# Reordering the start-up of a fused retention and gMLP kernel: the first v, the bias, the gain, the norms and the first fillers

## The chip, the cores and the metric

The kernel runs on one core of one Trainium2 chip. The metric is the device time of one execution in microseconds, as the median of several executions. The core has five engines that run side by side and wait for each other by semaphores: PE (TensorE, matmul; its weight loads are listed as PEld), DVE (VectorE), ACT (ScalarE), POOL (GpSimd) and SP (SyncE, which here only issues DMAs). Each engine works through its own instructions in program order. DMAs are issued from the instruction streams of SP, ACT and POOL.

## What is computed

Inputs q, k and v have 8 batches, 8 heads, 576 positions and 64 columns a head, in float32. First comes retention, a causal attention without softmax, in which each head h decays with its own gamma; then a gMLP block over the joined heads (512 columns):

```python
scores = scale * np.matmul(q, k.transpose(0, 1, 3, 2))
gamma = 1.0 - 2.0 ** (-5.0 - np.arange(H, dtype=np.float32))
Dmat = np.where(rel >= 0, gamma[:, None, None] ** rel[None, :, :], 0.0)
x = np.matmul(scores * Dmat[None], v)          # heads joined: (8, 576, 512)
...
h = gelu(x @ w_in)                             # tanh form, 1024 columns
u, v = h[..., :512], h[..., 512:]
v_n = (v - mu) / np.sqrt(var + 1e-06) * g_ln
v_s = np.einsum('ts,bsd->btd', w_sg, v_n) + b_sg[None, :, None]
out = x + (u * v_s) @ w_out
```

So each position needs a normalized row v_n, the 576 positions of a batch are then mixed by w_sg with the bias b_sg, and the gated result goes through w_out.

## The kernel before

**Blocks.** The work is cut into 18 blocks j, two groups of four batches with nine blocks each. The first block of a group (j = 0 and 9) holds the first 64 positions of its four batches; each of the other eight holds 256 positions of one batch, so that each batch has two blocks. A block has two chunks c of 128 rows.

**Names.** For a block, in the order of the data:

- load(j) (line 76) issues the DMAs of k, q and v. For j = 0 each of the three is four transfers of 128 KB, one for each batch, and for x >= 2 they go out on ACT's queue instead of SP's. Three buffers of each kind are there (pool ld), so load(j + 3) waits for the casts of block j.
- cast(j, part, engine) (247) scales k or q by the decay and writes them in bfloat16, or copies v: kb, qb, vb (klead, vlead for a leading block).
- T(j, part) (266) transposes k or q on PE; ACT copies kT, DVE copies qT out of PSUM.
- Sc(j, g) (283) forms half of the masked scores; DVE multiplies by the mask (tile ret).
- Z(j, c) (305) adds a chunk to the running state of keys and values (zp, copied to zb); inter(j) (327) multiplies the queries by that state, intra(j) (340) adds the product of scores and v; ACT and DVE copy the result, transposed, into xT.
- V(j, c) (361) projects a chunk by the second half of w_in (hv) and ACT applies gelu (vg). Its norm has three steps, kept as functions: stats (374: mean and variance, rs, and vc = (vg - mean) * g on DVE), power (371: rs to the power -1/2 on POOL) and norm (388: vn = vc * rs on ACT; for the leading rows two halves, vnm). Ahead of the loop they are called by hand as stats_of[n], pow_of[n] and norm_of[n] with n = 2 * j + c; in the loop they follow two and four steps later by themselves.
- U(j, c) (407) projects by the first half of w_in and applies gelu (uT).
- W(b, c, half) (420) mixes the positions of batch b by w_sg: five matmuls over the four vn of that batch and the vnm, then a product with uT on DVE (gT). It can end only when all norms of its batch are there. O(p, m) (439) multiplies by w_out, adds x and stores 128 rows.

**Constants.** split_b (168) clears the two bias tiles wL and splits b_sg into three bfloat16 parts (bp); place_b(e) (188) sends these into wL[e] by three small DMAs of POOL's; fill_first (184) and fill_consts (179) set constant halves of vnm; load_w(j) (193) loads w_sg in five pieces, and for j = SB w_out, on POOL's queue; build_wT (200) transposes w_sg; build_g (216) spreads g_ln over all rows by a matmul with a column of ones (gp, copied by ACT to g_bc). spin(n) (224) issues n matmuls on a tile of zeros that nobody reads.

**Order.** The order is written out by hand: lines 480 to 597 interleave blocks 0 to 2 with the constants and start block 3, and from line 602 a loop over j = 3 to 17 goes on: block j's intra, V and U, the scores of block j + 1, the transposes of j + 2, the casts of j + 3 and the loads of j + 4.

**Fillers.** W and O are not called at fixed places. release(j) (465) runs at the end of the second block of a batch and queues that batch's 8 W and 4 or 5 O in the list wo, behind the first two entries still in it and mixed with the rest; run(n) (460) executes the next n entries, if there are any. The loop has four such places for each block (line 601), 3 to 6 entries a block in all. What is left after the loop runs at the end (642).

Of the kernel before, what the change touches and what calls it, by code (L numbers as in the profile page):

```python
# [19 lines left out]
def kernel(  # L20
# [12 lines left out]
    nc = tc.nc  # L33
# [10 lines left out]
    SB = (S + 127) // 128  # L44
# [31 lines left out]
    def load(j, parts=(k, q, v)):  # L76
        if j not in loaded:
            loaded[j] = ld.tile([128, 2, H, 2, D], F32, name="qk"), ld.tile([128, H, 2, D], F32, name="vf")
        qk, vf = loaded[j]
        gr, b, half = place(j)  # L80
        for dst, src in ((qk[:, 1], k), (qk[:, 0], q), (vf, v)):
            if src not in parts:
                continue
            if b is None:
                for x in range(GB):
                    eng = nc.scalar if j == 0 and x >= 2 else nc.sync
                    eng.dma_start(dst[32 * x:32 * x + 32], src[GB * gr + x, :, :LEAD, :].rearrange(
                        "h (p a) d -> p h (a d)", a=2))
            else:
                s0 = LEAD + 256 * half  # L90
                nc.sync.dma_start(dst[:], src[b, :, s0:s0 + 256, :].rearrange("h (p a) d -> p h (a d)", a=2))
# [76 lines left out]
    def split_b():  # L168
        nc.gpsimd.memset(wL[0][64:], 0.0)
        nc.gpsimd.memset(wL[1][:64], 0.0)  # L170
        rest = bs
        for n in range(3):
            nc.gpsimd.tensor_copy(bp[:, n, :], rest[:])
            if n < 2:
                left = w3.tile([SB * 2, 64], F32, name="left")
                nc.gpsimd.tensor_tensor(left[:], rest[:], bp[:, n, :], op=Alu.subtract)
                rest = left

    def fill_consts():
        for x in (1, 2):  # L180
            nc.gpsimd.memset(vnm[x][0][64:], 1.0)
            nc.gpsimd.memset(vnm[x][1][:64], 1.0)

    def fill_first():
        nc.gpsimd.memset(vnm[0][0][64:], 1.0)
        nc.gpsimd.memset(vnm[0][1][:64], 1.0)

    def place_b(e):
        for n in range(3):
            r = 64 * (1 - e) + n  # L190
            nc.gpsimd.dma_start(wL[e][r:r + 1, :], bp[:SB * 2 - 1, n, :] if e else bp[1:, n, :])

    def load_w(j):
        if j == SB:
            nc.gpsimd.dma_start(w_out[:], moe_w_out.rearrange("(c p) f -> p c f", p=128))
            return
        n = min(128, S - 128 * j)
        nc.gpsimd.dma_start(wnat[:n, j, 64:64 + S], moe_w_sg[128 * j:128 * j + n, :])
# [17 lines left out]
    def build_g():  # L216
        gp = psD.tile([128, F2], F32, name="gp", tag="d")
        nc.tensor.matmul(gp[:], one[:], grow[:], start=True, stop=True)
        nc.scalar.copy(g_bc[:], gp[:])
# [4 lines left out]
    def spin(n):  # L224
        for _ in range(n):
            nc.tensor.matmul(idle[:], fill[:, :128], fill[:], start=True, stop=True)  # L226
# [20 lines left out]
    def cast(j, part, eng):  # L247
        s = blk.setdefault(j, {})
        qk, vf = loaded[j]
        b, half = place(j)[1:]  # L250
        kind = 0 if b is None else 1 + half
        if part == "q":
            dst, src, tab = w2.tile([128, 2, H, D], BF, name="qb"), qk[:, 0], gq
        else:
            pool = consts if b is None else w3
            dst = pool.tile([128, 2, H, D], BF, name=part + ("lead" if b is None else "b"))
            src, tab = (qk[:, 1], gk) if part == "k" else (vf[:], None)
        s[part + "b"] = dst
        o = dst[:].rearrange("p a h d -> p h a d")
        if tab is None:  # L260
            copy(eng, o, src)
        else:
            eng.tensor_tensor(o, src, tab[:, kind].rearrange("p a h -> p h a").unsqueeze(3).to_broadcast(  # L263
                [128, H, 2, D]), op=Alu.mult)
# [40 lines left out]
    def Z(j, c):  # L305

        gr, b, half = place(j)
        if b is None or (half, c) == (1, 1):
            nb = GB * gr if b is None else b + 1
            if c == 0 or nb == GB * (gr + 1):  # L310
                return
            src, lo, n, first = blk[NPG * gr], 32 * (nb % GB), 32, True
            zcur[0] = psZ.tile([128, KK, D], F32, name="zp")
        else:
            src, lo, n, first = blk[j], 64 * c, 64, False
        z, rows = zcur[0], slice(lo, lo + n)
        for a in range(2):
            for kk in range(KK):
                for r in range(2):
                    h = 2 * kk + r  # L320
                    nc.tensor.matmul(z[64 * r:64 * r + 64, kk, :], src["kb"][rows, a, h, :], src["vb"][rows, a, h, :],  # L321
                                     start=(first and a == 0 and kk == 0), stop=True, skip_group_check=True)
        zb = w3.tile([128, KK, D], BF, name="zb")
        copy(nc.scalar if j < 3 else nc.vector, zb[:], z[:])
        zbs[(j, 1) if c == 0 else (j + 1, 0)] = zb

    def inter(j):
        s = blk[j]
        qT = s["qT"]
        s["ot"] = ot = [psO.tile([128, KK, 2, 64], F32, name="ot") for _ in range(2)]  # L330
        if place(j)[1] is None:
            return
        for kk in range(KK):
            for c in range(2):
                for r in range(2):
                    rr = slice(64 * r, 64 * r + 64)
                    nc.tensor.matmul(ot[c][rr, kk], zbs[j, c][rr, kk, :], qT[rr, :, kk, 64 * c:64 * c + 64],  # L337
                                     start=(kk == 0), stop=False, skip_group_check=True)
# [20 lines left out]
    stats_of, pow_of, norm_of = {}, {}, {}  # L359
# [47 lines left out]
    def U(j, c):  # L407
        p, m = chunk(j, c)
        if p not in uTs:
            uTs[p] = pairp.tile([128, KK, NT * 128], BF, name="uT")  # L410
        hu = psD.tile([128, KK, 128], F32, name="hu", tag="d")
        for c in range(KK):
            for kk in range(KK):
                nc.tensor.matmul(hu[:, c, :], w_in[:, kk, 128 * c:128 * c + 128],  # L414
                                 xTs[p][:, kk, 128 * m:128 * m + 128],
                                 start=(kk == 0), stop=(kk == KK - 1), skip_group_check=True)
        nc.scalar.activation(uTs[p][:, :, 128 * m:128 * m + 128], hu[:], Act.Gelu_apprx_tanh)  # L417
        tick()
# [41 lines left out]
    def run(n):  # L460
        for _ in range(n):
            if wo:
                wo.pop(0)()

    def release(j):
        b, half = place(j)[1:]
        if b is None or half == 0:
            return
        ws = [lambda b=b, c=c, h=h: W(b, c, h) for h in range(2) for c in range(KK)]
        os = wo[2:]  # L470
        del wo[2:]
        while ws or os:
            wo.extend(ws[:2] + os[:1])
            ws, os = ws[2:], os[1:]
        p, e = divmod(b, 2)
        for m in ([MID] if e else []) + [(MID + 1) * e + x for x in range(MID)]:
            wo.append(lambda p=p, m=m: O(p, m))
# [2 lines left out]
    HEAD = 3  # L480
    spin(16)
    build_masks()
    split_b()
    cast(0, "k", nc.vector)
    T(0, "k")
    spin(2)
# [1 line left out]
    T(0, "q")  # L488
    spin(3)
    cast(0, "v", nc.gpsimd)  # L490
    place_b(0)
    Sc(0, 0)
    Sc(0, 1)
    Z(0, 1)
# [5 lines left out]
    intra(0)  # L500
    load(3)
    nc.gpsimd.memset(wnat[:, :, 0:64], 0.0)
    cast(1, "q", nc.vector)
    spin(3)
    V(0, 0, None)
    V(0, 1, None)
    T(1, "k")
    T(1, "q")
    cast(1, "v", nc.gpsimd)
    build_g()  # L510
    Sc(1, 0)
    Z(1, 0)
    cast(2, "k", nc.gpsimd)
# [16 lines left out]
    V(1, 1, None)  # L530
    Z(2, 0)
    inter(2)
    stats_of[0]()
    place_b(1)
    cast(3, "k", nc.gpsimd)
    fill_first()
    pow_of[0]()
    Sc(2, 1)
    Z(2, 1)
    wb = ["L0", "L1"] + list(range(SB - 1))  # L540
    U(0, 0)
    stats_of[2]()
    U(0, 1)
    intra(2)
    U(1, 0)
    stats_of[3]()
    pow_of[2]()
    norm_of[0]()
    norm_of[2]()
    V(2, 0, None)  # L550
    V(2, 1, None)
    cast(3, "q", nc.gpsimd)
    load_w(SB)
    load(5)
    build_wT(wb[0])
    cast(3, "v", nc.gpsimd)
    U(1, 1)
    build_wT(wb[1])
    stats_of[4]()
    pow_of[3]()  # L560
    fill_consts()
    pow_of[4]()
    norm_of[3]()
    build_wT(wb[2])
    U(2, 0)
    build_wT(wb[3])
# [4 lines left out]
    U(2, 1)  # L571
    build_wT(wb[5])
    norm_of[5]()
    T(3, "k")
    T(3, "q")
    release(2)
    cast(4, "k", nc.gpsimd)
    cast(4, "q", nc.gpsimd)
    cast(4, "v", nc.gpsimd)
    load(6)  # L580
    run(1)
    Sc(3, 0)
    Z(3, 0)
    run(1)
# [7 lines left out]
    cast(5, "q", nc.gpsimd)  # L592
    cast(5, "k", nc.gpsimd)
    cast(5, "v", nc.gpsimd)
    later(14, stats_of[1])
    later(16, pow_of[1])
    later(18, norm_of[1])
# [75 lines left out]
```

## Time and profile before

| | us |
|---|---|
| median of three executions | 238.41 (238.07 to 238.46) |
| the profiled execution | 236.13 |
| its span, first to last instruction | 234.4 |
| PE busy | 219.7 (94%) |
| DVE busy | 164.2 (70%) |
| ACT busy | 134.7 (57%) |
| POOL busy | 130.6 (56%) |
| moved by DMA | 41.58 MB, 177 GB/s on the mean |

The profiled execution is one of its own, faster by 2.28 us than the median of the three. Its span leaves out 1.7 us around the first and last instruction. A row of the timeline, as quoted below, has the start in us from the span's start, the length of the row (several instructions may be merged), the engine, the line of the kernel, the operation, the tiles written and read, the shapes, and in brackets how long the engine sat idle before it and what ended that. A row of the chain of waits has start, length and what the end of the kernel hung on at that time. A row of DMA issues has the queue, the number of transfers, the KB of each, and the us from issue to landing.

### The profile page before, as it was taken

The numbers are of one execution on the slowest core, as the hardware profiler recorded it, in microseconds if no ns is written. First come the engines' busy times: TensorE is split into PE (matmuls) and PEld (weight loads), VectorE is DVE, ScalarE is ACT, GpSimd is POOL, SyncE is SP. The second block draws the span as 40 slices with busy tenths as digits, with TensorE's granted clock in tenths as the row PEclk, the third lists the DMA queues.
The fourth block names the chain that finished last, engine by engine and source line by source line (L and its number), as shares of the span: only waits on it lengthen the run. The fifth ranks groups of instructions, "written<-read, shape, count | busy, mean of one in ns | idle before, by whom it ended". The sixth has DMA issues, their size and how long they took to land.

```text
span 234.4 us, 8354 instructions
## 1 busy us (share of the span) xinstructions
PE 219.7 (94%) x3604; PEld 157.1 (67%) x3604; DVE 164.2 (70%) x357; ACT 134.7 (57%) x217; POOL 130.6 (56%) x130
## 2 busy tenths in 40 slices
PE   7769889869999999999999999999999999999993
PEld 2425457758776777777777678777777777757651
DVE  5533767978889798668867778767876787648310
ACT  2524457844467764838475856757374838575142
POOL 7387956889758493819374665929291611113000
PEclk9958799999999999999999999999999999999999
DMA  7999999999901699278919797295903101311235
GB/s 170 303 286 309 308 261 279 262 276 242 289 17 48 192 221 262 49 236 227 265 47 268 197 299 187 48 275 155 277 20 137 46 6 24 113 52 40 89 116 201
DMA packets 64260, 41.58 MB, mean 177 GB/s; under 512 B 2208, under 2 KB 58592, under 8 KB 64224
## 3 DMA queue, kind: packets, MB, share of 16 engines
q1 hardware_dynamic: 61120, 39.07, 62.0%
q0 software_dynamic: 1472, 1.20, 3.1%
q10 hardware_dynamic: 1632, 0.79, 1.5%
q8 instruction: 28, 0.46, 0.9%
q14 instruction: 8, 0.07, 0.1%
HBM read 32.79 MB, written 9.44 MB: 180 GB/s over the span
## 4 chain that ended last, share of the span: by engine, by line
PE 73%; DVE 9%; ACT 6%; DMA 5%; POOL 4%; issue 1%; POOLq 1%; ACTq 0%; DVEq 0%
PE wp L434 14%; PE op L443 13%; PE hv L365 11%; PE hu L414 9%; PE tp L272 5%; PE ot L348 4%; PE op L446 3%; PE sc L296 3%; PE zp L321 3%; PE ot L337 3%; DMA vf<-in_v_dram 3%; PE idle L226 3%; DVE bst L376 2%; DMA qk<-in_q_dram 2%; DVE ret L300 2%; POOL rs L372 2%
## 5 line engine op out<-in xcount | busy, mean ns | idle before, releaser
L372 POOL TENSOR_TENSOR rs<-rs,mhalf 128x1 f32<-128x1 f32 x36 | 33.3, 926 | 74.9 <-DVE rs L380 73.2
L300 DVE TENSOR_TENSOR ret<-sc,mask 128x512 bf16<-128x512 f32 x72 | 46.2, 684 | 10.4 <-PE sc L296 10.4
L434 PE MATMUL wp<-wT,vn 128*128 128x288 bf16 x256 | 41.7, 287 | 0.1
L436 DVE TENSOR_TENSOR gT<-wp,uT 128x288 bf16<-128x288 f32 x64 | 28.2, 452 | 15.9 <-PE wp L434 14.3
L414 PE MATMUL hu<-xT,w_in 128*128 128x128 bf16 x576 | 37.8, 219 | 0.0
L365 PE MATMUL hv<-w_in,xT 128*128 128x512 bf16 x144 | 36.5, 380 | 1.1 <-ACT xT L245 1.1
L443 PE MATMUL op<-w_out,gT 128*128 128x512 bf16 x144 | 37.0, 380 | 0.0
L414 PEld LDWEIGHTS <-w_in 128*128 128x128 bf16 x576 | 34.1, 98 | 2.0
L368 ACT ACTIVATE vg<-hv 128x512 f32<-128x512 f32 x36 | 21.4, 597 | 21.2 <-PE hv L365 21.2
L397 ACT ACTIVATE vn<-vc,rs 128x512 bf16<-128x512 f32 x32 | 23.1, 722 | 18.2 <-POOL rs L372 17.9
L263 POOL TENSOR_TENSOR kb<-qk,gk 128x1024 bf16<-128x1024 f32 x16 | 31.2, 1948 | 3.1 <-DMA qk<-in_k_dram 3.1
L449 ACT COPY ob<-op 128x512 f32<-128x512 f32 x36 | 21.0, 588 | 18.8 <-PE op L446 13.1
L385 DVE SCALAR_TENSOR_TENSOR vc<-vg,mv,g_bc 128x512 f32<-128x512 f32 x36 | 29.5, 819 | 1.1 <-ACT vnm L393 1.1
L376 DVE BATCH_NORM_STATS2 bst<-vg 128x6 f32<-128x512 f32 x36 | 24.8, 689 | 7.3 <-ACT vg L368 6.8
L263 POOL TENSOR_TENSOR qb<-qk,gq 128x1024 bf16<-128x1024 f32 x15 | 28.9, 1927 | 0.0
L434 PEld LDWEIGHTS <-vn 128*128 128x128 bf16 x256 | 23.6, 98 | 7.8 <-ACT vn L397 0.5
L417 ACT ACTIVATE uT<-hu 128x512 bf16<-128x512 f32 x36 | 21.7, 602 | 12.4 <-PE hu L414 12.4
L245 ACT CAST xT<-ot 128x512 bf16<-128x512 f32 x33 | 22.0, 733 | 5.4 <-PE ot L348 5.4
L245 ACT COPY kT<-tp 128x1024 bf16<-128x1024 bf16 x18 | 18.1, 1004 | 5.6 <-PE tp L272 5.6
L365 PEld LDWEIGHTS <-xT 128*128 128x128 bf16 x144 | 13.0, 98 | 11.9 <-ACT xT L245 2.0
L443 PEld LDWEIGHTS <-gT 128*128 128x128 bf16 x144 | 12.6, 98 | 9.2
L434 PE MATMUL wp<-wL,vnm 128*128 128x288 bf16 x64 | 18.3, 288 | 0.0
(95 smaller groups left out, 297.1 us busy)
## 6 DMA issues: line engine op xcount, KB each, us to landing
qk<-in_k_dram SPq DMA_DIRECT2D x16, 512.0 KB, 7.7
qk<-in_q_dram SPq DMA_DIRECT2D x16, 512.0 KB, 6.7
vf<-in_v_dram SPq DMA_DIRECT2D x16, 512.0 KB, 7.5
out_dram<-ob SPq DMA_DIRECT2D x32, 256.0 KB, 2.6
wst<-in_moe_w_in_dram SPq DMA_DIRECT2D x2, 1024.0 KB, 8.0
out_dram<-ob SPq DMA_DIRECT2D x8, 128.0 KB, 2.8
qk<-in_k_dram SPq DMA_DIRECT2D x6, 128.0 KB, 4.1
qk<-in_q_dram SPq DMA_DIRECT2D x6, 128.0 KB, 4.3
```

The source lines that it names most:

```text
L245: (eng.copy if eng is nc.scalar else eng.tensor_copy)(o, i)
L263: eng.tensor_tensor(o, src, tab[:, kind].rearrange("p a h -> p h a").unsqueeze(3).to_broadcast([128, H, 2, D]), op=Alu.mult)
L300: nc.vector.tensor_tensor(s["ret"][:, r, 2 * g:2 * g + 2], sc[r][:], msk[:].unsqueeze(1).to_broadcast([128, 2, 2, 128]), op=Alu.mult)
L365: nc.tensor.matmul(hv[:], xTs[p][:, kk, 128 * m:128 * m + 128], w_in[:, kk, F2:], start=(kk == 0), stop=(kk == KK - 1))
L372: nc.gpsimd.tensor_tensor(st["rs"][:], st["rs"][:], mhalf[:], op=Alu.pow)
L376: nc.vector.bn_stats(bst[:], vg[:])
L385: nc.vector.scalar_tensor_tensor(vc[:], vg[:], mv[:, 0:1], g_bc[:], op0=Alu.subtract, op1=Alu.mult)
L397: nc.scalar.mul(vn[:], vc[:], rs[:])
L414: nc.tensor.matmul(hu[:, c, :], w_in[:, kk, 128 * c:128 * c + 128], xTs[p][:, kk, 128 * m:128 * m + 128], start=(kk == 0), stop=(kk == KK ...
L434: nc.tensor.matmul(ps[:], vns[p, m][e][:, 128 * c:128 * c + 128], w, start=(x == 0), stop=(x == SB - 1))
L436: nc.vector.tensor_tensor(gTs[p][:, c, col:col + HS], ps[:], uTs[p][:, c, col:col + HS], op=Alu.mult)
L443: nc.tensor.matmul(op[:], gTs[p][:, c, r], w_out[:, c, :], start=(c == 0), stop=False, skip_group_check=True)
```

## The change

Only the order of the work ahead of the loop and one queue are changed; no computation is added or dropped.

```diff
-                    eng = nc.scalar if j == 0 and x >= 2 else nc.sync
+                    eng = nc.scalar if j == 0 and x >= 2 and src is not v else nc.sync
...
     build_masks()
-    split_b()
     cast(0, "k", nc.vector)
...
     cast(0, "v", nc.gpsimd)
-    place_b(0)
+    split_b()
     Sc(0, 0)
...
     nc.gpsimd.memset(wnat[:, :, 0:64], 0.0)
+    place_b(0)
     cast(1, "q", nc.vector)
-    spin(3)
+    build_g()
     V(0, 0, None)
...
     cast(1, "v", nc.gpsimd)
-    build_g()
+    spin(2)
     Sc(1, 0)
...
     inter(2)
+    fill_first()
     stats_of[0]()
-    place_b(1)
-    cast(3, "k", nc.gpsimd)
-    fill_first()
     pow_of[0]()
     Sc(2, 1)
     Z(2, 1)
+    cast(3, "k", nc.gpsimd)
     wb = ["L0", "L1"] + list(range(SB - 1))
     U(0, 0)
+    norm_of[0]()
     stats_of[2]()
+    pow_of[2]()
     U(0, 1)
     intra(2)
     U(1, 0)
+    norm_of[2]()
     stats_of[3]()
-    pow_of[2]()
-    norm_of[0]()
-    norm_of[2]()
+    cast(3, "q", nc.gpsimd)
+    pow_of[3]()
     V(2, 0, None)
     V(2, 1, None)
-    cast(3, "q", nc.gpsimd)
-    load_w(SB)
     load(5)
     build_wT(wb[0])
-    cast(3, "v", nc.gpsimd)
+    norm_of[3]()
     U(1, 1)
     build_wT(wb[1])
     stats_of[4]()
-    pow_of[3]()
-    fill_consts()
+    cast(3, "v", nc.gpsimd)
+    place_b(1)
     pow_of[4]()
-    norm_of[3]()
     build_wT(wb[2])
...
     norm_of[5]()
+    release(2)
+    run(1)
     T(3, "k")
     T(3, "q")
-    release(2)
     cast(4, "k", nc.gpsimd)
     cast(4, "q", nc.gpsimd)
     cast(4, "v", nc.gpsimd)
+    load_w(SB)
     load(6)
-    run(1)
+    run(2)
     Sc(3, 0)
...
     cast(5, "v", nc.gpsimd)
+    fill_consts()
     later(14, stats_of[1])
```

All four transfers of the first v now go out on SP's queue, ahead of the second half of w_in. On POOL the split of b comes behind the copy of the first v, place_b(0) behind the clearing of wnat, place_b(1) behind block 3's copy of v, w_out's DMA behind block 4's casts and fill_consts behind block 5's. The product that spreads g is issued while the first xT are copied, in the place of three fillers on zeros, and two such fillers stand in its old place. Each norm follows its statistics and power sooner. The first batch is released ahead of T(3), one filler runs there and two instead of one behind it: six entries of wo run ahead of the loop instead of four.

## The prediction

> **What bounds the kernel now.** I read the page's busy times first, then busy time by stretches of time cut where the granted clock changes (columns: start and end, length, busy us of PE, PEld, DVE, ACT and POOL with their instruction counts, granted clock, DMA share, GB/s).
>
> ```profile
> 9.46:12.87 3.41, 1.58 (x38) 0.83 (x36) 2.17 (x4) 0.58 (x1) 0.81 (x4) 1.00 1.13 328
> 12.87:16.28 3.41, 2.41 (x21) 1.22 (x21) 0.74 (x2) 1.32 (x2) 3.41 (x5) 0.50 1.21 290
> 16.28:19.69 3.41, 3.41 (x39) 1.40 (x37) 0.15 (x1) 0.20 (x1) 3.28 (x4) 0.50 1.21 288
> ...
> 26.52:29.93 3.41, 2.93 (x39) 1.82 (x43) 2.51 (x3) 1.38 (x2) 2.93 (x5) 0.50 1.21 245
> ...
> 55.50:209.10 153.60, 152.54 (x2762) 114.38 (x2761) 119.92 (x260) 98.03 (x158) 86.75 (x67) 1.00 0.59 156
> ```
>
> From 55.5 to 209.1 PE is busy 152.54 of 153.60 us at full clock: the loop is bound by PE, and whatever is won or lost before it is carried through. The change edits only what precedes the loop, so three things count: when the loop begins, which fillers (W and O, one queue) it finds, and what is left after it. The chain of waits tells what leads up to there:
>
> ```profile
> 6.26 6.37 DMA vf<-in_v_dram
> ...
> 13.87 0.64 PE zp L321 x10
> 14.51 3.95 PE idle L226 x9
> 18.46 1.00 PE ot L348 x21
> 19.46 0.89 PE idle L226 x3
> 20.34 1.83 PE hv L365 x8
> 22.18 0.90 PE tp L272 x16
> 23.07 1.06 PE gp L218 x2
> ...
> 27.00 1.01 PE tp L272 x8
> ```
>
> The last quarter of the first v, issued by ACT at 6.26, lands 6.37 us later, at 12.63. Everything up to 27 hangs on it: the value states, nine fillers at half clock, the first value projections.
>
> **First v on one queue.** Now two quarters go out on SP and two on ACT, with half of w_in right behind on SP:
>
> ```profile
> 3.98 0.81 SPq L87 DMA_DIRECT2D vf<-in_v_dram  x2
> 5.17 0.40 SPq L139 DMA_DIRECT2D wst<-in_moe_w_in_dram  x1
> ```
>
> ```profile
> wst<-in_moe_w_in_dram SPq DMA_DIRECT2D x1, 1024.0 KB, 6.7
> vf<-in_v_dram SPq DMA_DIRECT2D x2, 128.0 KB, 4.4
> ```
>
> Four quarters on SP at 0.4 each, the last held by one earlier landing, put the last issue at about 5.2; with SP's 4.4 to landing that is 9.6, and I take 9.9 as it stands behind three others. Bounds: 9.6, and 12.63 if it gains nothing. w_in is issued 0.8 later and lands at 12.7 instead of 11.9; POOL's copy of it started at 15.3, so that is hidden. [...]
>
> **POOL in the head.** The split of b leaves its place before v's copy (first two stretches: POOL column) and goes behind it; place_b(0) moves from 13.77 to behind the clearing at 18.22.
>
> ```profile
> 4.17:5.35 1.18, 1.18 (x4) 0.43 (x3) 0.00 (x0) 0.29 (x2) 1.14 (x2) 1.00 1.14 259
> 7.96:10.33 2.37, 1.48 (x14) 0.77 (x14) 1.37 (x2) 1.30 (x3) 2.07 (x5) 1.00 1.05 363
> ```
>
> ```profile
> 12.78 1.04 POOL L245 CAST vlead<-vf 128x1024 bf16<-128x1024 f32 x1 [2.46 <-DMA vf<-in_v_dram]
> 13.77 1.58 POOL L191 DMA_DIRECT2D wL<-bp  x3
> 15.34 1.05 POOL L495 CAST w_in<-wst 128x1024 bf16<-128x1024 f32 x1
> 16.34 1.94 POOL L263 TENSOR_TENSOR kb<-qk,gk 128x1024 bf16<-128x1024 f32 x1
> 18.22 0.37 POOL L502 MEMSET wnat<- 128x320 bf16 x1
> 18.52 1.04 POOL L245 CAST vb<-vf 128x1024 bf16<-128x1024 f32 x1
> 20.92 2.23 POOL L263 TENSOR_TENSOR kb<-qk,gk 128x1024 bf16<-128x1024 f32 x1 [1.36 <-DMA qk<-in_k_dram]
> ```
>
> New order from 10.0: 1.04 + (1.18 + 2.37) + 1.05 + 1.94 + 0.37 + 1.58 + 1.04 = 10.6, with some 0.5 of gaps 21.1. There k of block 2 has just landed (20.9), so POOL is back on its old timetable: the 3.55 and 1.58 lie in the old waits of 2.46 and 1.36 and in v's 2.7, and that cover is used up. What comes earlier is w_in's copy (by 15.8 done), kb(1) (17.8); what comes later is vb(1), at 21.1 instead of 19.6.
>
> **PE in the head.** Z(0,1) follows the copy at 11.1 to 11.4 instead of 13.87. Nine fillers take 3.95 at half clock, about 2 at full. The product for g (1.06) replaces three fillers (0.89) behind intra(0) and hides beside the xT copies, apart from some 0.2; the two fillers set where it stood are waited out beside the copy of kT. The two V take 1.83 from about 16 to 17 on, T(1) follows by 19 to 20, and Z(1,0) waits for vb(1) at 21.1. Then:
>
> ```profile
> 24.30 0.35 PE L321 MATMUL zp<-vb,kb 64*64 64x64 bf16 x12
> ```
>
> From Z(1,0) to T(2,k) at 27.00 were 2.7 us; 21.1 + 2.7 is 23.8, also past kb(2) at 23.3 (21.1 + 2.23). **T(2,k) gains 3.2.** Bounds: 3.8 with v at its earliest, 0 with v at 12.63 (then POOL reaches kb(2) at 23.8, and T(2,k) follows at 26 to 27). Up to U(0,0) the order is kept, and the gain with it.
>
> **Statistics, norms, powers.**
>
> ```profile
> 35.41 1.96 PE L414 MATMUL hu<-xT,w_in 128*128 128x128 bf16 x32
> ```
>
> ```profile
> 39.47 1.44 ACT L393 ACTIVATE vnm<-vc,rs 64x512 bf16<-64x512 f32 x2
> ...
> 48.51 0.72 ACT L397 ACTIVATE vn<-vc,rs 128x512 bf16<-128x512 f32 x1 [0.45 <-POOL rs L372]
> ```
>
> ```profile
> 40.95 2.01 DVE L385 SCALAR_TENSOR_TENSOR vc<-vg,mv,g_bc 128x512 f32<-128x512 f32 x1 [1.08 <-ACT vnm L393]
> ```
>
> From U(0,0) to the end of the last norm (49.23) are 13.8 us. The first norm, 1.44 on ACT, moves ahead of U(0,1)'s activation and of block 2's xT copy: V(2,0) comes up to 1.4 later. In exchange DVE no longer waits 1.08 for that norm, nor is that vc drawn out to 2.01. I take −0.2, bounds −1.3 and +1.4. place_b(1) moves on POOL from under the old wait for k(3) to between v(3)'s copy and a power; the copy of w_out and the constants' memsets, 2.9 together, move behind block 4's and block 5's casts. T of those blocks comes at least 2 us after its casts, which is the cover; without it the whole 2.9 would be lost.
>
> **One W ahead of T(3), two behind it.**
>
> ```profile
> 50.18 0.42 PE L296 MATMUL sc<-qT,kT 64*64 64x128 bf16 x16 [0.28 <-ACT kT L245]
> ```
>
> ```profile
> 55.51 0.64 PE L348 MATMUL ot<-ret,vb 64*64 64x128 bf16 x32
> ```
>
> The first W needs the last norm, and T(3,k), T(3,q) are now queued behind it on PE. Sc(3,0) came 0.95 after that norm (50.18); now W's rest 0.4, two T of 0.45 and two W (1.23) give 2.5, and one more product on DVE 0.2: **+1.8**, bounds +1.2 and +2.5. In it lie two W that used to come later. Loop begins (intra(3), 55.51): −3.2 − 0.2 + 1.8 = **−1.6**.
>
> **The fillers in the loop.** release(2) queues 8 W and 4 O. Before, 4 are run ahead of the loop, 6 in blocks 3 and 4, and 2 O are left in front of the next batch; now 6 are run ahead and none is left. So the first W of batch 1 stands where this O stood:
>
> ```profile
> 75.71 1.04 PE L443 MATMUL op<-w_out,gT 128*128 128x512 bf16 x4
> ```
>
> ```profile
> 76.85 0.72 ACT L397 ACTIVATE vn<-vc,rs 128x512 bf16<-128x512 f32 x1
> ```
>
> Its last matmul needs that norm, done at 77.57; four of five matmuls run until 76.2. **+1.4**, bounds 0 and +1.9. At the later releases one or two O are left and the W come one O (1.08) further on, which their norms meet.
>
> **After the loop.**
>
> ```profile
> 215.21 0.73 ACT vn L397
> ...
> 217.98 1.23 PE wp L434 x10
> 219.21 0.86 PE op L443 x4
> 220.07 0.22 PE op L446 x4
> ```
>
> Two W less (1.23) remain after the last V, and while its norm is awaited two O run where two shorter W ran, which closes some 0.4 of idle time: **−1.6**, bounds −2.2 and −0.5.
>
> **Sum** against the profiled execution: −3.2 − 0.2 + 1.8 + 1.4 − 1.6 = **−1.8**, so 236.13 becomes 234.3 (its span 234.4 with 1.7 around it becomes 232.6). The median shown is 238.41, 2.3 above that execution; the difference carried over gives **236.6**.
>
> **Rivals.** (A) *Clock stays full.* In the stretches above the grant fell after one with PE 1.58 of 3.41 busy, and again to 0.50 at 26.52. If the fuller new head avoids the second fall, half of that stretch's 2.93, 1.4 us, is saved as well: 235.2. [...] (B) *v lands no earlier*, the change not doing what it says: SP's queue is backed up too. The head gains 0, the rest is −0.2 + 1.8 + 1.4 − 1.6 = +1.4: 239.8. Against it speaks the 4.4 of SP's own quarters. (C) *Slower by the clock.* From 12.87 on the grant stays at half until past T(1), because g's one-row product and a few small matmuls follow the spins. Then 12 + 3.95 + 1.0 (intra) and, at twice their times in the chain, 2.1 (g), 3.7 (V), 1.8 (T), with the old 1.2 from T(1)'s end at 23.08 to Z(1,0), put Z(1,0) at 25.8, 1.5 later than before. The head is +1.5 instead of −3.2, the sum +2.9: 241.3. It decides if the stretch up to 16.28, then filled, doesn't bring the clock back. For it: 2.41 of 3.41 busy wasn't enough. Against: 3.41 of 3.41 was. (D) *Half the gain goes under on POOL*: vb(1), kb(2) and the loads of w_sg slip by 1.6; the sum is −0.2, 238.2, no change.
>
> **Numbers.** Forecast 0.50, A 0.17, D 0.12, B 0.12, C 0.09. The forecast's own range is 235.3 to 238.0. From A's far side to B's: 233.6 to 239.8, which leaves out C and a rest below. Less than 0.2% (0.5 us) can't be told from no change. Faster: A and nearly all of the forecast, 0.67; same: D, 0.12; slower: B, C, 0.21.
>
> **What would show it.** v's copy on POOL at about 10 and Z(0,1) by 11.5, without a wait for DMA; T(2,k) near 23.8; the last norm near 46; intra(3) near 54; a PE wait of over 1 us on the first W of batch 1; two fillers fewer after the last V. It is wrong if v's last quarter still lands after 12, if the granted clock is half where the first V run, or if a cast on POOL delays T(4) or T(5).

## The result, and the profile after

| | before | after |
|---|---|---|
| median of 13 runs each, one chip | 238.07 us | 235.10 us |
| ratio after to before, 95% interval | | 0.990 (0.9865 to 0.9934) |
| the same ratio, a later chip job | 236.15 us (29 runs) | 235.16 us (12 runs), 0.996 (0.991 to 1.000) |
| profiled execution, span | 236.13, 234.4 | 234.34, 232.6 |
| mean granted clock in it | 0.978 | 0.995 |
| PE busy | 219.7 | 215.0 |

In the first comparison the change made the kernel faster by 1%, clear of the noise; in the second by 0.4%, with an interval that reaches up to no change. The ratios leave out the runs that are over 1.5% above the fastest of their kernel (24 of the 81 of before in the three later jobs, 23 of them with a mean clock below 0.980, and 2 of the 25 of after), so they are not the quotients of the medians. The span came out at 232.6, where the sum had put it, but not by the terms of the sum. This table sets the starts of the same work side by side (us, from the timelines):

| | before | after | difference |
|---|---|---|---|
| T(2,k) | 27.00 | 22.78 | -4.2 |
| U(0,0) | 35.41 | 30.85 | -4.6 |
| end of the last norm ahead of the loop | 49.23 | 44.64 | -4.6 |
| intra(3), begin of the loop | 55.51 | 52.52 | -3.0 |
| where batch 1's first W stands | 75.71 | 73.15 | -2.6 |
| V(17,1) | 210.00 | 208.89 | -1.1 |
| end of the last matmul | 230.35 | 227.60 | -2.75 |
| end of the span | 234.4 | 232.6 | -1.8 |

Busy time of the kernel after by the same stretches (columns as in the prediction: start and end, length, busy us of PE, PEld, DVE, ACT, POOL, granted clock, DMA share, GB/s):

```profile
10.00:22.78 12.78, 10.42 (x199) 5.92 (x198) 8.24 (x12) 6.16 (x10) 11.15 (x17) 1.00 1.18 310
22.78:30.85 8.07, 6.27 (x140) 3.79 (x140) 5.89 (x11) 4.04 (x6) 6.39 (x10) 1.00 1.13 286
30.85:44.64 13.79, 11.41 (x174) 8.74 (x169) 11.84 (x26) 10.95 (x20) 10.91 (x11) 1.00 1.03 265
44.64:52.52 7.88, 7.23 (x141) 5.90 (x141) 6.21 (x13) 1.97 (x2) 7.87 (x6) 1.00 1.09 269
52.52:73.15 20.63, 20.42 (x444) 15.45 (x442) 17.76 (x38) 13.13 (x23) 17.20 (x16) 1.00 0.81 211
73.15:208.89 135.74, 133.14 (x2329) 99.22 (x2324) 102.63 (x224) 85.51 (x137) 70.70 (x55) 1.00 0.57 153
208.89:227.60 18.71, 18.71 (x159) 12.59 (x157) 7.68 (x18) 8.13 (x14) 1.84 (x2) 1.00 0.29 94
```

The granted clock is 1.00 in all of these stretches, where in before it was 0.50 from 12.87 to 19.69 and from 26.52 to 29.93. PE is now idle for 1.8 of the 8.07 from T(2,k) to U(0,0). DMA is as busy as before up to U(0,0) (a share of 1.18 and 1.13, where before had 1.17 from 10 to T(2,k) and 1.14 from there to U(0,0)), and what landed late in the head lands late again: k of block 2 at 20.73 (20.85 in before), w_in's second half at 27.38 (26.86), k of block 3 at 32.22 (31.12). POOL's row behind the first v, by the timeline of after:

```profile
10.26 1.04 POOL L245 CAST vlead<-vf 128x1024 bf16<-128x1024 f32 x1 [6.14 <-DMA vf<-in_v_dram]
11.36 0.57 POOL L169 MEMSET wL<- 64x576 bf16 x1
...
12.50 0.23 POOL L173 CAST bp<-bs 10x64 bf16<-10x64 f32 x1
...
18.97 1.04 POOL L245 CAST vb<-vf 128x1024 bf16<-128x1024 f32 x1 [0.18 <-DMA vf<-in_v_dram]
20.80 1.93 POOL L263 TENSOR_TENSOR kb<-qk,gk 128x1024 bf16<-128x1024 f32 x1 [0.79 <-DMA qk<-in_k_dram]
```

v's copy starts at 10.26 (last quarter landed at 10.11), the value rows of block 1 are cast by 20.0, and POOL then waits 0.79 for k of block 2 again. That landing is now the floor of the head: the cast of this k runs from 20.80 to 22.73, and T(2,k), which PE had waited 0.77 for, starts at 22.78. The timelines of ACT and PE of after:

```profile
27.40 1.04 ACT L527 CAST w_in<-wst 128x1024 bf16<-128x1024 f32 x1 [2.02 <-DMA wst<-in_moe_w_in_dram]
```

```profile
22.78 0.62 PE L272 MATMUL tp<-ident,kb 128*128 128x128 bf16 x8 [0.77 <-POOL kb L263]
...
29.75 0.47 PE L337 MATMUL ot<-qT,zb 64*64 64x128 bf16 x10 [1.53 <-ACT zb L245]
...
44.69 0.30 PE L434 MATMUL wp<-wT,vn 128*128 128x288 bf16 x1 [1.51 <-ACT vn L397]
```

ACT stands still 2.02 for the second half of w_in, which landed at 27.38; the gelus of V(1,0) and V(1,1) and the copy zb wait behind that copy in ACT's order, and PE waits 1.53 for zb. That is the first place where a wait came in for the one removed. The W ahead of T(3) waits 1.51 for the last norm.

### The profile page after: what moved, and what is told of

Read it like the earlier page. It is cut to its first block, busy times and chain, and to the rows that moved or that the text cites. A ratio compares the mean times of both kernels' runs of the same rounds, so it can differ in the third digit from the quotient of the medians.

```text
span 232.6 us, 8357 instructions
## 1 busy us (share of the span) xinstructions
PE 215.0 (92%) x3603; PEld 154.8 (67%) x3603; DVE 165.8 (71%) x357; ACT 134.7 (58%) x217; POOL 129.4 (56%) x130
## 4 chain that ended last, share of the span: by engine, by line
PE 67%; ACT 7%; DVE 6%; DMA 6%; POOL 5%; SPq 5%; issue 1%; ACTq 1%; DVEq 0%; POOLq 0%
PE wp L434 15%; PE op L443 13%; PE hv L365 10%; PE hu L414 10%; PE tp L272 5%; SPq L91 5%; DMA wst<-in_moe_w_in_dram 4%; PE op L446 3%; POOL rs L372 3%; PE zp L321 3%; PE sc L296 3%; PE ot L348 3%; PE ot L337 3%; DMA qk<-in_q_dram 2%; DVE bst L376 2%; ACT vnm L393 2%
```

## The experiments

Ratios are to the kernel before, run beside each kernel; the kernel before was at 236.7, 236.2 and 237.5 in the three jobs (e1 to e4; e5, e7 to e9; e10 to e13), the kernel after at 235.10 and 235.16 in its two. Ratios of different jobs therefore do not have the same base, and differences of some tenths of a per cent between jobs decide nothing.

### The queue alone, and the queue without the rest

e1, the kernel before with one part of the change:

```diff
-eng = nc.scalar if j == 0 and x >= 2 else nc.sync
+eng = nc.scalar if j == 0 and x >= 2 and src is not v else nc.sync
```

> The kernel before with one edit: all four quarters of the first v on SP's queue. Theory (the head gain comes from v's last quarter alone, the reorder of POOL's start-up is not needed for it): v's copy on POOL at about 10.3 instead of 12.78, T(2,k) at 22.5 to 23.5 instead of 27.00, intra(3) some 4 us earlier than 55.51, and since no filler moves, no wait on the first W of batch 1 and the end as long as before: span about 230.5, 4 us less than before, 2 us less than the changed kernel (232.6). Rival (the split behind v's copy is needed too, because POOL is the bound of the head): place_b(0) still stands before w_in's copy, POOL is late, T(2,k) comes at 25 or later and the span stays at 232.5 or above.

Measured: 235.61, ratio 0.998 (0.994 to 1.002), span 232.7. T(2,k) came at 22.68, as in after: the whole gain of 4.3 up to there is the queue's, and moving the split of b, place_b and the product for g added nothing to it, since in e1 too T(2,k) waited (0.59) for the cast of block 2's k, which started at 20.69 as its data landed. The theory's other numbers were missed: intra(3) came 2.6 earlier (52.90) and not 4, and the span was not 230.5. Part of the gain was lost again (the clock was at half from 22.70 to 26.11 as well). From U(0,0) (31.21) to the end of the last norm (46.61) were 15.4 instead of 13.8. POOL's timeline in e1, and in after:

```profile
31.89 1.93 POOL L263 TENSOR_TENSOR kb<-qk,gk 128x1024 bf16<-128x1024 f32 x1 [2.63 <-DMA qk<-in_k_dram]
...
34.94 1.09 POOL L372 TENSOR_TENSOR rs<-rs,mhalf 128x1 f32<-128x1 f32 x2
```

```profile
29.60 0.65 POOL L372 TENSOR_TENSOR rs<-rs,mhalf 128x1 f32<-128x1 f32 x1
32.29 1.93 POOL L263 TENSOR_TENSOR kb<-qk,gk 128x1024 bf16<-128x1024 f32 x1 [2.04 <-DMA qk<-in_k_dram]
```

In the old order the first power stands behind the cast of block 3's k, whose data landed at 31.12 in before and at 32.22 in after, and for which POOL waited until 31.89 in e1. So the first power came at 34.94, the time it had in before (34.87). In after it stands ahead of that cast.

e5, the kernel after with that line put back:

> The kernel after, with the first v again half on SP's queue and half on ACT's; all else as after. Theory (the early v buys the early T(2,k), but w_in's second half, which landed at 27.38 in after, is a floor behind it that had swallowed 2.02 of that gain): v's copy ends near 13.7 instead of 11.3, POOL's row of work behind it is 2.4 later, T(2,k) comes at 25 instead of 22.78, ACT's wait for w_in shrinks from 2.02 to nearly nothing, and U(0,0) comes only 0.5 to 1.0 later than 30.85; span 233.1 to 233.8 against 232.6, ratio to the kernel before 0.990 to 0.996. Rival (nothing is swallowed, the whole 2.5 goes through to the end): U(0,0) at 33.3, span 235, ratio at or above 1.000. If the granted clock falls in the head, up to 2 us more for either.

Measured: 238.59, ratio 1.011 (1.006 to 1.016), span 236.8; slower than before, so in the new order the early v is needed. U(0,0) came at 35.36. By its number that is the rival's 33.3 with the 2 that a fall of the clock may add, but v landed later than both had assumed, and from T(2,k) (28.32) to U(0,0) were 7.0 instead of 8.1: the 1.0 that the landing of w_in had swallowed was there again. v's last quarter landed at 14.52 (10.11 in after, 12.63 in before), and this (timelines of POOL and of PE in e5) followed:

```profile
14.68 1.04 POOL L245 CAST vlead<-vf 128x1024 bf16<-128x1024 f32 x1 [10.55 <-DMA vf<-in_v_dram]
```

```profile
15.77 0.64 PE L321 MATMUL zp<-vlead,klead 32*64 32x64 bf16 x16 [4.29 <-POOL vlead L245]
16.73 3.51 PE L226 MATMUL idle<-fill 128*128 128x512 bf16 x8 [0.33 <-issue]
```

The clock was at half from 13.17 to 20.00 in that profile, and eight fillers took 3.51, where nine took 2.12 in after; the late v and the half clock came together.

### The order of the norms

e10 is e1 with the order of after from fill_first to place_b(1), w_out's DMA where before has it, and fill_consts behind place_b(1):

```diff
-    stats_of[0]()
-    place_b(1)
-    cast(3, "k", nc.gpsimd)
     fill_first()
+    stats_of[0]()
     pow_of[0]()
     Sc(2, 1)
     Z(2, 1)
+    cast(3, "k", nc.gpsimd)
...
     cast(3, "v", nc.gpsimd)
+    place_b(1)
     fill_consts()
     pow_of[4]()
```

> The kernel before with the first v on SP's queue, and with the order of statistics, powers, norms and block 3's casts that after has; split of b, g, W and O, w_out's DMA stay as in before. Theory (POOL's first power stood behind the cast of block 3's k, whose data land at 32 however early the head is; with the power ahead of it the statistics follow the head): the first power at about 30 instead of 34.94, the stage from U(0,0) to the end of the last norm 13.5 to 14.1 instead of the 15.40 that it took with the queue alone, intra(3) 51.0 to 51.8 instead of 52.90, span 230.8 to 232, ratio 0.988 to 0.994. Rival (the order of the norms is worth nothing, as the profiles of before and after, 13.82 and 13.79, make it look): stage 15 or more, intra(3) at 52.5 or later, ratio 0.997 or above.

Measured: 234.71, ratio 0.989 (0.983 to 0.994), a ratio as the theory had it, but the stage took 16.2, intra(3) came at 53.41 and the span was 232.9, so none of its times held. Its first step did. The timelines of POOL, ACT and PE in e10:

```profile
29.28 0.94 POOL L372 TENSOR_TENSOR rs<-rs,mhalf 128x1 f32<-128x1 f32 x1 [0.24 <-DVE rs L380]
...
42.92 0.52 POOL L182 MEMSET vnm<- 64x512 bf16 x1
43.41 1.09 POOL L372 TENSOR_TENSOR rs<-rs,mhalf 128x1 f32<-128x1 f32 x2
```

```profile
44.01 0.72 ACT L397 ACTIVATE vn<-vc,rs 128x512 bf16<-128x512 f32 x1 [3.72 <-POOL rs L372]
```

```profile
45.42 1.01 PE L272 MATMUL tp<-ident,qb 128*128 128x128 bf16 x8 [1.06 <-ACT wT L245]
```

The first power came at 29.28, and norm 3 ended 2.9 earlier than in e1 (38.60 instead of 41.52). Then the fourth power stood behind place_b(1) and the four memsets, 3.8 of POOL's time (39.61 to 43.41). ACT's fourth norm waited 3.72 for it, T(3,q) waited 1.06 for the copy of wT behind that norm, and the clock fell too (43.68 to 50.51). So the new order lets the first norms follow an early head, and gives that back where the constants stand in front of a later power; what the order alone is worth in time was not measured.

### W and O

e4, the kernel before with release(2) and one W ahead of T(3) and run(2) behind it:

```diff
     norm_of[5]()
+    release(2)
+    run(1)
     T(3, "k")
     T(3, "q")
-    release(2)
...
-    run(1)
+    run(2)
```

> The kernel before with the early fillers alone: release(2) and one W ahead of T(3), two behind. Theory: intra(3) 1.6 later than 55.51, a wait of 1.4 on the first W of batch 1, 1.6 less after the last V: about +1.4, span 235.8, ratio to before about 1.006. Rival (the early W are free or a gain): span 234.4 or below.

Measured: 238.54, ratio 1.009 (1.004 to 1.013), span 237.3: slower, and by 2.9 where the three terms (1.8 + 1.4 - 1.6) made 1.6; 0.9 of the rest came at the very end, as in after (see the terms below). PE's timeline in e4 at batch 1's first W:

```profile
77.92 0.30 PE L434 MATMUL wp<-wL,vnm 128*128 128x288 bf16 x1
78.05 0.53 PE L434 MATMUL wp<-wT,vn 128*128 128x288 bf16 x3
79.84 0.30 PE L434 MATMUL wp<-wT,vn 128*128 128x288 bf16 x1 [1.25 <-ACT vn L397]
```

It took 2.22 instead of 0.77. intra(3) came 1.9 later, 0.3 of it there before the last norm, the tail from V(17,1) to the last matmul was 1.6 shorter.

e2, the kernel after with those lines as in before:

> The changed kernel with release(2) again behind T(3) and one filler instead of two behind it: four fillers ahead of the loop, as before. Theory (the early W cost more than they bring): intra(3) 1.6 us earlier than 52.52, no wait of 1.4 on the first W of batch 1, the stretch after the last V 1.6 longer again; together 1.4 less, span about 231.2, ratio to before about 0.984. Rival (the two W fill time that PE would wait anyway): intra(3) at most 0.4 earlier, span 232.6 or above, ratio 0.990 or above.

Measured: 234.18, ratio 0.993 (0.988 to 0.997), span 231.8, between both. intra(3) came at 50.48, 2.0 earlier than in after, and the first W took 0.77; yet 2 us went again in block 3. Timelines of POOL, DVE and PE in e2:

```profile
55.59 0.52 POOL L182 MEMSET vnm<- 64x512 bf16 x1
56.08 1.93 POOL L263 TENSOR_TENSOR qb<-qk,gq 128x1024 bf16<-128x1024 f32 x1
57.97 1.02 POOL L372 TENSOR_TENSOR rs<-rs,mhalf 128x1 f32<-128x1 f32 x1
```

```profile
55.84 2.71 DVE L385 SCALAR_TENSOR_TENSOR vc<-vg,mv,g_bc 128x512 f32<-128x512 f32 x1
```

```profile
59.21 0.61 PE L272 MATMUL tp<-ident,kb 128*128 128x128 bf16 x8 [1.55 <-DVE ret L300]
```

With the loop begun earlier, the four memsets behind block 5's casts push POOL's cast of q(6) onto DVE's product vc, which takes 2.71 where it took 1.11 in after; the masked scores come late, and T(5,k) waits 1.55 (the expectation of e9 calls it T(4,k)).

e3, the kernel after with two entries fewer run in blocks 3 and 4, so that two O stay in front of batch 1:

```diff
-    share = {3: 3, 4: 3, 9: 5, 10: 4, 11: 4, 17: 5}
-    where = {6: (2, 1, 1, 2), 5: (2, 1, 1, 1), 4: (2, 0, 1, 1), 3: (1, 0, 1, 1)}
+    share = {3: 2, 4: 2, 9: 5, 10: 4, 11: 4, 17: 5}
+    where = {6: (2, 1, 1, 2), 5: (2, 1, 1, 1), 4: (2, 0, 1, 1), 3: (1, 0, 1, 1), 2: (1, 0, 1, 0)}
```

> The changed kernel, six fillers ahead of the loop, but two instead of three in each of blocks 3 and 4, so that two O stand in front of batch 1 again. Theory (the 1.4 us of the first W of batch 1 is a wait for its last norm, and O in front of it hide it): that W takes 0.8 instead of 2.2, intra(3) stays at 52.5, blocks 3 and 4 are two O (2.2) shorter and the end is 1.6 longer again; together about 1.4 less, span about 231.2. Rival (the wait only moves: blocks 3 and 4 need three fillers to cover their own waits): the wait goes, but PE idles 1 us or more in blocks 3 and 4, span 232.3 or above.

Measured: 233.50, ratio 0.987 (0.982 to 0.991), span 231.5; the first W took 0.78. The stall is the missing O's, and is cured without giving up the W ahead of T(3).

### The clock

e7, the kernel before with fillers in PE's wait for v, and e13, the kernel after without the eleven fillers behind Z(0,1) and ahead of Sc(1,0):

```diff
     Sc(0, 1)
+    spin(14)
     Z(0, 1)
```

```diff
-    spin(9)
     inter(0)
...
-    spin(2)
     Sc(1, 0)
```

> The kernel before with 14 more matmuls on zeros between the scores of block 0 and Z(0,1), about 3.0 us at full clock, where PE waits 2.5 us for v's copy; nothing else is changed. They compute nothing that is read. Theory (a good part of the gain is the granted clock, which fell in the kernel before behind the stretch with PE busy 1.58 of 3.41 and stays full in after): the clock stays full from about 6 us on, the nine fillers behind Z(0,1) take 2.0 instead of 3.95, T(2,k) comes at 24.0 to 24.9 instead of 27.00, span 231.8 to 232.8 against 234.4, ratio 0.990 to 0.995, and the times spread less than the 234 to 239 of the kernel before. Rival (v's landing alone sets the head, the clock is only a symptom): T(2,k) at 26.5 or later, span 234 or more, ratio 0.998 or above.

> The kernel after without the nine matmuls on zeros ahead of inter(0) and the two ahead of Sc(1,0). They compute nothing that is read. Theory (the gain of after stands mostly in the granted clock, and the clock falls after a stretch of 3.41 with PE busy half of it, without any single wait of 3 us): the clock goes to half somewhere between 13 and 20 in the profile, mean granted clock about 0.98 over the runs, ratio 0.999 or above, although intra(0) can come 1.2 earlier. [...]

Measured, e7: 234.27, ratio 0.991 (0.988 to 0.995), span 232.5. The order and the queues of before, with a clock of 0.995 on the mean of its runs, gain as much as the change. The number for T(2,k) was missed (26.82): in the profiled execution the clock fell once, from 11.03 to 14.44, under the fillers themselves, which took 4.08 and held Z(0,1) back to 16.21. But it did not fall behind T(2,k), and from there to U(0,0) were 7.3 instead of 8.4.

Measured, e13: 235.88, ratio 0.994 (0.990 to 0.997), span 234.4. The clock fell in the profile and was 0.98 on the mean, as the theory had it, and the profiled execution was as long as that of before. But the ratio is not the theory's 0.999: it cannot be told from the 0.990 and 0.996 of after. v is still early in e13, which may be why the time did not go all the way back; this is not shown. Busy time of e13 by stretches, and PE's row with the longest wait in the first of them:

```profile
10.48:13.89 3.41, 1.44 (x50) 1.09 (x50) 2.47 (x4) 1.90 (x3) 3.07 (x7) 1.00 1.14 339
13.89:17.31 3.42, 3.35 (x34) 1.44 (x34) 1.87 (x3) 0.98 (x2) 3.37 (x5) 0.50 1.23 293
```

```profile
13.36 0.21 PE L348 MATMUL ot<-ret,vlead 64*64 64x128 bf16 x1 [1.35 <-DVE ret L300]
```

No wait in that stretch is longer than 1.35, PE is busy 1.44 of its 3.41, and in the next the clock is at 0.50.

e8, the kernel after once more:

> The kernel after once more, unchanged, beside the others of this call. 0.990 of the kernel before, with its interval of 0.987 to 0.993, is expected again if the share of the clock is the same on this chip; nearer to 1 if the kernel before keeps its full clock more often here.

Measured: 235.16, ratio 0.996 (0.991 to 1.000). This profile had a fall of the clock. PE's timeline and the stretches around it:

```profile
31.23 0.47 PE L337 MATMUL ot<-qT,zb 64*64 64x128 bf16 x10 [2.53 <-ACT zb L245]
```

```profile
29.12:32.53 3.41, 1.30 (x50) 1.17 (x51) 1.76 (x5) 2.09 (x5) 2.42 (x4) 1.00 1.17 271
32.53:35.95 3.42, 3.42 (x44) 3.22 (x45) 3.35 (x6) 2.17 (x4) 2.23 (x2) 0.50 0.84 222
```

w_in's second half landed at 28.86 there, PE waited 2.53 for zb, and U(0,0) then ran at half clock. So the wait that had come in for v's (1.53 in after, at full clock) was followed in this execution by a stretch at half clock; the span was 234.6.

The clock over the runs that stand in the ratios (before in the three jobs; after in both of its own):

| mean granted clock of the run | before | after |
|---|---|---|
| 0.990 or more | 21 runs, median 235.35 | 16 runs, median 235.05 |
| 0.980 to 0.990 | 21 runs, 235.78 | 7 runs, 235.42 |
| below 0.980 | 15 runs, 237.54 | none |

In the rows that both have, the kernels differ by 0.3 to 0.4 us; the rest of the gain goes with the last row, in which after has no runs. This sorts runs by their clock; it does not show what moved the clock.

### Mending what came in its place

e11, the kernel after with ACT's half of the w_in copy behind inter(2):

```diff
-    for n in range(2):
-        (nc.gpsimd.tensor_copy if n else nc.scalar.copy)(w_in[...], w_stage[0][...])
+    nc.gpsimd.tensor_copy(w_in[:, :, 256:512], w_stage[0][:, :, 256:512])
...
     inter(2)
+    nc.scalar.copy(w_in[:, :, 0:256], w_stage[0][:, :, 0:256])
```

> The kernel after with one line moved: ACT's half of the copy of w_in's second half from ahead of V(1,0) to behind inter(2). Theory (ACT stood still 2.02 there for a DMA that lands at 27 to 29, and the gelus and the state's copy behind it, which have their data, waited with it): PE's wait for zb at inter(2) 0.6 or less instead of 1.5 to 2.5, U(0,0) about 0.7 earlier, fewer falls of the clock behind that wait, ratio 0.988 to 0.993 where after itself has 0.990 and 0.996. Rival (U(0,0) needs that copy anyway, so the wait only moves on): U(0,0) at 30.8 or later, ratio 0.995 or above.

Measured: 234.64, ratio 0.991 (0.987 to 0.995), span 232.8. PE's wait for zb was 0.53, and from T(2,k) to U(0,0) were 7.1 instead of 8.1; but the stage up to the last norm took 0.7 more (14.45), and the clock was no fuller (0.990). 0.5 us in the medians, within the interval: alone, the move gives most of it back.

e9, the kernel after with that move, W as in before (e2), and the constants in POOL's wait for k of block 3:

```diff
     pow_of[0]()
+    fill_consts()
...
     cast(5, "v", nc.gpsimd)
-    fill_consts()
```

> The kernel after with its W in the place of before (none ahead of T(3), one behind it), with ACT's half of the w_in copy moved from ahead of V(1,0) to behind inter(2), and with the constants' memsets (four of 0.52) moved from behind block 5's casts to behind the first power, where POOL waited 2.04 for k of block 3. Theory: the first W of batch 1 does not stall (0.8 instead of 2.2), PE's wait of 1.3 for zb at inter(2) shrinks to 0.5 or less, T(4,k) does not wait 1.55 for the scores' product on DVE as it did where the W alone were put back, since the power is no longer behind the memsets; U(0,0) at 29.7 or earlier, intra(3) near 49.5, span 228.5 to 230, ratio 0.975 to 0.983. Rival (PE has no slack left there: k of block 3, landing at 32, and the DMAs in flight set the stage, so that each mended wait comes back further on): span 231 or more, ratio 0.987 or above.

Measured: 232.08, ratio 0.981 (0.976 to 0.986), span 230.4. W took 0.77, zb was awaited 0.53, T(5,k) was not held. From intra(3) to the end were 179.3, 2.0 less than in e2; 1.55 of that is the wait that went with the constants' new place. U(0,0) at 31.03, intra(3) at 51.10 and the span missed their numbers, as the clock was at half up to just ahead of V(1,0), which came at 26.6. Busy time of e9 by stretches:

```profile
18.72:22.13 3.41, 1.94 (x80) 1.62 (x80) 2.09 (x4) 0.64 (x2) 2.56 (x2) 1.00 1.19 285
22.13:25.55 3.42, 2.73 (x38) 1.84 (x43) 1.91 (x3) 1.12 (x2) 3.42 (x7) 0.50 1.06 374
```

e12 is e9 with eight fillers in waits:

```diff
-    spin(2)
+    spin(4)
     Sc(1, 0)
...
+    spin(3)
     T(2, "k")
...
+    spin(3)
     V(2, 0, None)
```

> The kernel with the three mends (0.981 in its own run, span 230.4 with the clock at half from 22.13 to 25.55) with eight more matmuls on zeros where PE waits: two more ahead of Sc(1,0), three ahead of T(2,k) (a wait of 0.77 for POOL), three ahead of V(2,0) (0.80 for ACT). Theory (the remaining fall follows a stretch with short waits, and filling them keeps the clock): clock full in the head, mean 0.996 or more, span 229 to 230, ratio 0.974 to 0.979. Rival (the fillers push the work behind them, and gain nothing): span 230.4 or more, ratio 0.981 or above.

Measured: 230.97, ratio 0.974 (0.970 to 0.979), span 229.0, clock 0.999 on the mean of its runs; all as the theory had it. U(0,0) came at 29.88, intra(3) at 49.96. Row of the page of e12 (granted clock by 40 slices of the span):

```profile
PEclk9999999999999999999999999999999999999999
```

By the times of two jobs it is 1.8% faster than after (230.97 against 235.16), and the best kernel here.

## Why the prediction was right, and where it was not

The direction and the span were right (span 232.6 in both). The time was 235.1 instead of 236.6, just under the forecast's own range of 235.3 to 238.0 and beside rival A's 235.2. The terms:

- **T(2,k), -3.2 with 3.8 as the best:** -4.2. The mechanism held: v's last quarter at 10.11 (9.9 predicted), POOL's wait for k of block 2 back. The mis-sized term is POOL's row: the split was counted at 3.55 and took 2.7, its first cast 0.23 where it had 1.03 in before (last section). So Z(1,0) came at 20.06 and not 21.1, and what held T(2,k) was the other bound, the cast of block 2's k: it ended at 22.73 and not 23.3, as it took 1.93 and not 2.23. The 2.7 from Z(1,0) to T(2,k) came out again, but 0.77 of it is PE's wait for that cast. And e1 showed that POOL's reordering, on which the working spent most, earned nothing at this point.
- **"Up to U(0,0) the order is kept, and the gain with it":** this step failed. V(1,0) came 5.6 earlier (25.44 instead of 31.01), and 1.0 of it ended in ACT's wait for w_in; in e8 more. That landing (27.38), and that of k(3) (32.22), are floors that the earlier head ran into. The second was disarmed by the order of the norms, the first was not.
- **Norms, -0.2:** 13.79 instead of 13.82, nothing. Right as a size between the two profiles, but the working missed what the step is for: without it (e1) the stage grows by 1.6 with the early head.
- **One W ahead of T(3), +1.8:** +1.6 in after and in e4 (7.88 and 7.87 from the last norm to intra(3), 6.28 in before). **First W of batch 1, +1.4:** +1.4 in both. **Tail, -1.6:** -1.6 to the last matmul in both. These three held. Missing were 0.4 in blocks 3 and 4, and 0.9 at the very end. Blocks 3 and 4 now run two W and four O where they ran four W and two O, which the working put at nothing: PE is busy 20.42 of 20.63 from intra(3) to batch 1's first W, and was busy 19.70 of 20.20 there in before. The chain of waits ends with ACT's copy, in after and in before:

```profile
227.69 0.59 ACT ob L449
```

```profile
230.43 0.58 ACT ob L449
```

From its end to the end of the span are 4.3 in after and 3.4 in before. All six kernels whose tail has the two fillers less (after, e4, e5, e8, e11, e13) have 4.6 to 5.0 from the last matmul to the end, the other eight 4.0. The last store lands 2.4 to 3.0 after its issue in the six (3.0 in after) and 2.0 in the others; why is open.

- **The sum** was right by luck: the head came 1.4 earlier at intra(3) than it had it, and what follows cost 1.4 more.
- **Constants and w_out at nothing:** the cover that was named held in after, and e2 showed its price when the loop begins 2.0 earlier: T(5,k) waits 1.55.
- **From the execution to the median, +2.3:** this is where the time itself was off by 1.5. The working carried the gap of before over to after; by the table of clocks that gap goes mostly with the clock, and after loses it less often; its execution was 0.76 below its median.
- **Rival A** came true in its premise, the clock stays full, and in its price of 1.4 for the second fall: from T(2,k) to V(1,0) were 2.66 instead of 4.01. It was no extra on top of the sum, as ACT's wait for w_in took 1.0 of it back before U(0,0). In e7 the same price is 1.1 (8.4 less 7.3 from T(2,k) to U(0,0)), and there the clock without an early v gives 0.991, as much as the change. **B** fell with the landing at 10.11; e5 has B's condition and more (v at 14.52), and was 1.1% slower than before. **C** and **D** did not come: the clock was full, and U(0,0) kept all that T(2,k) had gained.

The gain of the early v and that of the clock do not add up: e7 has only the clock (0.991), e13 the early v with the clock of before (0.994), and after both (0.990 and 0.996). These intervals overlap, so either alone may bring all of the gain; how the 0.4 to 1% splits between them stays open.

## What to carry to other kernels

Where a transfer holds the head back, ask which landing is next: here v came 2.52 earlier, and the head moved as far as k of block 2 (20.73) and w_in's second half (27.38). Look which copies wait for it ahead of work that has its data: with ACT's copy of w_in behind inter(2), PE's wait for zb was 0.53 instead of 1.53 (e11), though the time gained by that move alone stayed within the interval. Before reordering a start-up, fill PE's waits there and look at the granted clock of many runs: that alone gave 0.991 in e7, and a single profile can't tell the two causes apart. An entry taken from a queue of fillers is missed where the queue runs dry: the first W of batch 1 took 2.22 instead of 0.77 in e4, which was slower than before (1.009).

## What the runs showed of the hardware

**The clock fell behind short waits too.** The stretches at half clock ahead of the last matmul lasted 3.41 or 6.8 us (26.52 to 29.93 and 12.87 to 19.69 in before, 32.53 to 35.95 in e8, 22.13 to 25.55 in e9). The 3.41 us ahead of such a stretch had PE busy 1.30 (e8), 1.44 (e13), 1.58 (before), 1.67 (e7) and 1.94 us (e9), the longest single wait there being that for v in before (2.53, of which 1.52 by then) and 0.43 in e9; behind 1.78 in after (42.34 to 45.75) the clock stayed at 1.00. The second fall in before came behind 2.96, so busy time alone does not settle it, and what does is not shown.

**A product of DVE or POOL, and longer work on the other.** Timelines of POOL and DVE in before:

```profile
7.96 1.03 POOL L173 CAST bp<-bs 10x64 bf16<-10x64 f32 x1 [2.61 <-DMA bs<-in_moe_b_sg_dram]
9.08 0.29 POOL L176 TENSOR_TENSOR left<-bs,bp 10x64 f32<-10x64 f32 x1
9.44 0.23 POOL L173 CAST bp<-left 10x64 bf16<-10x64 f32 x1
```

```profile
7.68 1.22 DVE L263 TENSOR_TENSOR qb<-qk,gq 128x1024 bf16<-128x1024 f32 x1 [1.08 <-DMA qk<-in_q_dram]
```

The first of these casts took 1.03 with DVE's product of 1.22 under way, and ended 0.09 behind it; the second, of the same size, took 0.23, as did the first in after (12.50), where DVE was at the masked scores. In e2 it is the other way round: vc, which took 0.74 in before (at 45.00, with POOL at memsets), took 2.71 beside POOL's product of 1.93, and ended 0.54 behind it; in after the same vc took 1.11 and also ended 0.54 behind POOL's product. These rows show neither the cause nor which of the two goes first (in e2 DVE's row starts 0.24 ahead of POOL's, and its 2.71 ends later). The 0.80 between the two casts is most of what the prediction had too much for the split of b (3.55, and 2.7 in after).

**A wait that no engine ends.** In e1, e2, e3 and e9 a W in block 10 stood still 0.92, 0.40, 0.69 and 0.33 in mid-product, put down to issue; in before it did not. Nothing here shows its cause, and it is as large as the smaller terms of the sum.
